# Attention, soft mixture and second layer on one core: last tile's scores moved up, unread products taken out, loads paced earlier, running maximum kept per slot and place

## The chip, the cores and the metric

The kernel runs on one core of one Trainium2 chip. The metric is the device time of one execution in microseconds (us), as the median of the runs shown. The engines have short names: PE is TensorE (PEld its weight loads), DVE VectorE, ACT ScalarE, POOL GpSimd; SP is the engine that only issues transfers here. Each takes its instructions in the order of the program and waits on semaphores for the others. PSUM is the memory that PE writes, SBUF the large memory beside the engines.

## The reference

Three layers follow one another. Attention within chunks of 64 places, a soft mixture of 8 experts with 4 slots each (so 32 slots), and a layer with a softmax unit, a normalisation and two weights:

```python
scores = scale * q_c @ k_c^T; attn = softmax(scores); x = attn @ v_c      # 4608 tokens of 512
logits = x @ phi                                                          # 4608 x 32
d = exp(logits - logits.max(0)); d /= d.sum(0) + 1e-09                    # over the tokens
slot_input = d.T @ x                                                      # 32 x 512
slot_out[e] = relu(slot_input[e] @ w1[e]) @ w2[e]                         # 8 experts
c = softmax(logits, over the slots); x = c @ slot_out
h = x @ w_in; solu = h * softmax(h); out = layernorm(solu) * g_ln @ w_out
```

The maximum over all 4608 tokens is not known while they come; the kernel keeps a running maximum and multiplies the sums so far by the exponent of the difference (`al`) whenever a block of four tiles is added.

## The kernel before, in words

The 4608 tokens are 36 tiles of 128, and four tiles are a block (9 blocks). Tiles 0 to 33 run through a software pipeline of 34 steps. In step i the letters of a row of `STEP` (row i mod 4) say in which order the pieces of work are written, and so in which order each engine gets them: `S` (scores of tile i, 16 products), `mx` and `sub` (maximum and subtraction, DVE), `exp` (ACT), `PT` and `PTe` (transposes of the tile before and their copy out of PSUM by ACT), `x` (products with v of tile i-2), `rz`, `rc`, `xm` (row sums by ACT, reciprocal and multiplication by DVE), `xT` and `xTe` (transposes of tile i-3 and their copy by ACT). Letters `t`, `m`, `u`, `a`, `add`, `mul`, `sq` turn the second layer's weights from their raw form, and `qk`, `v`, `raw`, `W` issue loads on SP.

Once in four steps a block is folded in: `LT` makes the logits of four tiles in PSUM (32 slots by 4 places in the partitions, 128 tokens along the row), `lte` copies them to the SBUF tile `ltb`, `L` transposes them, `lall` stores them, `tm` takes the running maximum along the row, `mT` transposes that maximum, `mn`, `d`, `mc` (DVE) take the maximum over the four places, subtract it and pick it into a column, `de` (ACT) takes the exponent in place and `al` the factor for the older sums; `z` multiplies the exponents with ones on PE to get their sum, `sl` multiplies them with the tiles, and `acc` adds both to the running sums on DVE.

The expert weights are 64 loads of 512 KB on SP's queue. 23 of them have a place in `ring` from the start; `PACE[i]` says how many are issued by step i. The others go to places that other tiles leave (`own_c`, `own_q`, `own_v`, `own_p`, `own_t`, `own_x`) and to `ring` places that were used up.

Tiles 34 and 35 and everything up to the second layer are written out in `ORDER`: names with the operations they stand for, which are checked to come after what they need, and are otherwise issued as listed. `S34`, `S35` are the scores, `mx`, `sub`, `exp`, `PT`, `ptev`, `x`, `rz`, `ev`, `xT`, `xtev`, `LT` follow for each tile (tile 35 in two halves, 350 and 351; `ev` is reciprocal and multiplication). `lte8`, `L8`, `tm8`, `mT8`, `mn8` are the last block without its last tile, `lte83`, `Ls`, `L83`, `mnl` that tile; `mb` spreads the maximum, `d7`, `d8`, `de7`, `de8`, `sl70` to `sl81`, `z8`, `acc80`, `acc81`, `zt`, `si0`, `si1`, `siT` give the slots' inputs. `id0` to `id6` (line 646) are 13 instructions of products of the unit matrix with itself into PSUM places that nobody reads then; PE runs each of them in two passes.

Then the experts: `w1_000` to `w2_111` and `wc48` to `wc63` are PE's products with the 64 weight loads. Beside them the second layer is prepared: `cm0` and `cm1` are the mean of `w_out` on PE, `cme` its copy to SBUF on DVE, `cms0` to `cms7` subtract it on POOL (line 834), `px0` to `px7` take maxima of the results on DVE (line 1059), `px8` and `wmt` collect them (PE, line 1071), and `wmv`, `hi`, `lo` split the weights by that scale. `cz0` to `cz5` is the other softmax on DVE and ACT (lines 889 to 899). From about 187 us a loop over the 36 tiles runs the second layer with PE back to back to the end; nothing of it is touched.

## Time and profile before

| | before |
|---|---|
| median of 3 runs | 404.35 us (404.04 to 406.44) |
| the profiled execution | 406.2 us, of which 404.4 us span from first to last instruction |
| mean granted TensorE clock | 0.999 |
| PE busy in the span | 385.9 us (95%) |
| DVE, ACT, POOL busy | 311.5, 223.8, 199.4 us |
| transferred | 99.20 MB, of that 70.60 MB read from HBM |

The profile is one execution on the chip. Times in its rows count from the first instruction. A row of the timeline stands for one instruction or several merged ones, and says how long its engine sat idle before it and for whom. Ends of products on PE are modelled, so the start of the next row says more than a duration.

### The profile page before, as it was taken

What the parts mean: (1) busy time and instruction counts of PE and PEld (TensorE: products, weight loads), DVE (VectorE), ACT (ScalarE), POOL (GpSimd) and SP (SyncE); (2) the same over time, 40 slices, a digit from 0 to 9 for tenths busy, and PEclk for the clock granted to TensorE, in tenths of its full rate; (3) what the DMA queues carried; (4) which work ended last, traced back from release to release, by engine and by line L of the source; (5) the groups of instructions that cost most, each with busy time, mean ns of one, the idle gap of its engine ahead of it and who ended that gap; (6) DMA issues with size and microseconds to landing.
All of it is one profiled execution on the core that took longest, in us unless ns stands there. A gap on an engine that the chain in (4) does not pass through costs nothing. (4 is left out here: it accounts for less than half of the span.)

```text
span 404.4 us, 10343 instructions
## 1 busy us (share of the span) xinstructions
PE 385.9 (95%) x3961; PEld 223.0 (55%) x3961; DVE 311.5 (77%) x777; ACT 223.8 (55%) x470; POOL 199.4 (49%) x201
## 2 busy tenths in 40 slices
PE   3798999999999999999999999999999999999997
PEld 2676777877787752355544444444444444444445
DVE  3588788888987447683989789999888888888840
ACT  1487777877776512231576765556545545455521
POOL 2377677777778428240113235555545445454430
PEclk9999999999999999999999999999999999999999
DMA  7999999999999999993056756778657786567661
GB/s 231 361 411 409 407 407 408 409 397 387 403 361 347 404 398 402 408 410 82 15 98 151 130 134 140 166 166 160 144 132 135 156 130 143 133 143 156 131 157 52
DMA packets 101153, 99.20 MB, mean 245 GB/s; under 512 B 78064, under 2 KB 78704, under 8 KB 101104
## 3 DMA queue, kind: packets, MB, share of 16 engines
q1 hardware_dynamic: 101104, 98.54, 77.9%
q8 instruction: 31, 0.51, 0.5%
q14 instruction: 18, 0.15, 0.1%
HBM read 70.60 MB, written 9.44 MB: 198 GB/s over the span
## 5 line engine op out<-in xcount | busy, mean ns | idle before, releaser
L1197 POOL TENSOR_SCALAR uh<-u,sc 128x1024 f16<-128x1024 f32 (+1 forms) x35 | 65.0, 1857 | 51.2 <-issue 38.3
L1396 PEld LDWEIGHTS <-uhT 128*128 128x128 f16 x560 | 52.2, 98 | 68.6 <-issue 9.0
L1396 PE MATMUL o_ps<-xb,uhT 128*128 128x512 f16 x280 | 66.6, 380 | 0.8 <-DMA uhT<-uh 0.8
L1396 PE MATMUL o_ps<-xb,ulT 128*128 128x512 f16 x280 | 66.3, 379 | 0.0
L1396 PE MATMUL o_ps<-wo,uhT 128*128 128x512 f16 x280 | 66.1, 379 | 0.0
L1325 ACT ACTIVATE e<-h_ps,nm 128x1024 f32<-128x1024 f32 x34 | 37.8, 1112 | 43.9 <-DVE nm L1319 43.9
L1213 ACT ACTIVATE e<-u,nmean 128x1024 f32<-128x1024 f32 x35 | 40.1, 1147 | 28.7 <-DVE nmean L1212 28.7
L257 PE MATMUL s_ps<-qk 128*64 128x128 f32 x576 | 42.4, 291 | 10.8 <-DMA qk<-in_qkT 7.3
L1363 POOL TENSOR_TENSOR a<-a,mhalf 128x1 f32<-128x1 f32 x36 | 21.7, 604 | 56.6 <-DVE a L1380 42.7
L1319 DVE TENSOR_REDUCE nm<-h_ps 128x1 f32<-128x1024 f32 x34 | 41.5, 1220 | 9.7 <-PE h_ps L1314 9.7
L1188 DVE SCALAR_TENSOR_TENSOR u<-h_ps,e 128x1024 f32<-128x1024 f32 x35 | 42.8, 1223 | 6.1 <-ACT e L1325 6.1
L1396 PEld LDWEIGHTS <-ulT 128*128 128x128 f16 x280 | 27.3, 98 | 33.1 <-issue 0.3
L1373 DVE SCALAR_TENSOR_TENSOR ul<-u,sc,uh 128x1024 f16<-128x1024 f32 x35 | 45.3, 1295 | 0.0
L257 PEld LDWEIGHTS s_ps<-qk 128*64 128x64 f32 x576 | 33.1, 144 | 17.9 <-issue 12.1
L266 DVE TENSOR_REDUCE mx<-s_ps 128x8 f32<-128x512 f32 x36 | 24.7, 685 | 12.5 <-PE s_ps L257 12.3
L399 ACT ACTIVATE xt_b<-xt_ps 128x512 f32<-128x512 f32 (+1 forms) x37 | 21.5, 584 | 17.3 <-PE xt_ps L417 16.5
L220 POOL TENSOR_SCALAR conv<-conv 128x256 f32<-128x256 f32 x16 | 17.5, 1096 | 24.6 <-ACT conv L207 24.6
L1414 ACT ACTIVATE ob<-o_ps,a 128x512 f32<-128x512 f32 x35 | 23.7, 678 | 9.5 <-PE o_ps L1396 8.0
L1314 PE MATMUL h_ps<-s,c4T 128*128 128x512 f32 x68 | 27.6, 488 | 0.0
L278 ACT ACTIVATE p<-p 128x512 f32<-128x512 f32 x35 | 21.7, 620 | 6.7 <-DVE p L272 6.7
L272 DVE TENSOR_TENSOR p<-s_ps,mx 128x512 f32<-128x512 f32 x35 | 24.1, 690 | 0.9
L230 POOL TENSOR_TENSOR conv<-conv 128x256 int32<-128x256 int32 x32 | 23.3, 727 | 2.6
(234 smaller groups left out, 637.8 us busy)
## 6 DMA issues: line engine op xcount, KB each, us to landing
w<-in_w SPq DMA_DIRECT2D x45, 512.0 KB, 8.3
qk<-in_qkT SPq DMA_DIRECT2D x72, 256.0 KB, 7.0
vall<-in_v SPq DMA_DIRECT2D x18, 520.0 KB, 7.6
out<-ob SPq DMA_DIRECT2D x35, 256.0 KB, 2.1
raw<-in_w SPq DMA_DIRECT2D x16, 512.0 KB, 7.6
qk<-in_w SPq DMA_DIRECT2D x4, 512.0 KB, 9.6
w_raw<-in_w SPq DMA_DIRECT2D x3, 512.0 KB, 9.3
vall<-in_w SPq DMA_DIRECT2D x3, 512.0 KB, 9.0
```

The source lines that it names most:

```text
L257: nc.tensor.matmul(s[ts(c, 64), ts(g, 128)], b[:, 1, ts(2 * g + c, 64)], b[:, 0:3:2, ts(2 * g + c, 64)], start=True, stop=True, tile_posit ...
L266: mark("mx", nc.vector.tensor_reduce(out=mx, in_=s, axis=AX.X, op=ALU.max))
L272: mark("sub", nc.vector.tensor_tensor(out=p, in0=s, in1=mx.unsqueeze(2).to_broadcast([128, 8, 64]), op=ALU.subtract,))
L1188: nc.vector.scalar_tensor_tensor(out=u, in0=d["h"], scalar=1.0, in1=e, op0=ALU.mult, op1=ALU.mult, accum_out=zz[:, 1:2])
L1197: nc.gpsimd.tensor_scalar(out=uh[:, 0:n], in0=u[:, 0:n], scalar1=d["sc"][:, 1:2], scalar2=1.0, op0=ALU.mult, op1=ALU.mult)
L1213: nc.scalar.activation(out=d["e"], in_=d["u"], func=AF.Square, bias=nmean, scale=1.0, accum_out=d["zz"][:, 2:3])
L1314: nc.tensor.matmul(h[:, ts(n, 512)], c4T[:, i, :], s4[n], start=True, stop=True)
L1319: nc.vector.tensor_reduce(out=nm, in_=st[i]["h"], axis=AX.X, op=ALU.max, negate=True)
L1325: nc.scalar.activation(out=d["e"], in_=d["h"], func=AF.Exp, bias=d["nm"], scale=1.0, accum_out=d["zz"][:, 0:1])
L1373: nc.vector.scalar_tensor_tensor(out=ul, in0=d["u"], scalar=d["sc"][:, 1:2], in1=d["uh"], op0=ALU.mult, op1=ALU.subtract)
L1396: nc.tensor.matmul(d["o"], lt(n % 8), w(n % 8), start=(n == 0), stop=(n == 23))
L1414: nc.scalar.activation(out=ob, in_=d["o"], func=AF.Copy, scale=d["a"][:, 7:8])
```

## The change

Six things are done.

`S35`, the scores of tile 35, and `mx35` stand directly behind `S34` and `mx34`, and the list around them is reordered. The products `id0` to `id6` are gone. `PACE` is higher from its 19th number on.

In the pipeline the running maximum stays per slot and place: the block's logits are stored with their sign turned, `tm` becomes a minimum along the row into one of two columns in turn, and the exponent `e` is taken by ACT from `ltb` one step earlier, directly behind `lall`, with its sum `z` from the same instruction and with `al` behind it. PE then transposes the exponents (`eT`) where it transposed the maximum, and `de` is a copy out of PSUM. `mn`, `d`, `mc` on DVE and the product `z` on PE are gone in blocks 0 to 6.

The last two blocks need one maximum for the four places together. For that `ml` is stored, `ml4` on POOL spreads it over four columns by a mask `msk` (a DVE reduction at the start), and `mT8` gets one more product; a DVE maximum in `mn8` goes.

In `ORDER` `cm1` moves from ahead of `w1_000` to behind `w1_001`, and on DVE `d7` and `acc80` go ahead of `mc` and `zacc8`.

```diff
 PACE = [
-    0, 0, 1, 1, 2, 3, 3, 4, 4, 5, 6, 6, 7, 7, 8, 9, 9, 10, 10, 11, 12, 12, 13, 13, 14, 15, 15, 16,
-    16, 17, 18, 18, 19, 22, 25, 25,
+    0, 0, 1, 1, 2, 3, 3, 4, 4, 5, 6, 6, 7, 7, 8, 9, 9, 10, 11, 11, 12, 13, 14, 14, 15, 16, 16, 17,
+    18, 19, 19, 20, 21, 23, 25, 25,
...
-hz0 sl71 de8 al sl70 own_x z8 sl80 zacc8 sl81 zt acc80 acc81 zr si0 si1 siT open2 cm1 w1_000 w1_001 cme rl00 w1_010
+acc80 sl81 own_x zacc8 acc81 zt si0 si1 zr siT open2 w1_000 w1_001 cm1 cme rl00 w1_010 cz0 cms2 cms3 ht00 w1_011 he00
...
+    msk = kvp.tile([128, 4], F32, name="msk")
+    nc.vector.tensor_reduce(out=msk, in_=ident.rearrange("p (t s) -> p t s", t=4), axis=AX.X, op=ALU.add)
...
-    nc.gpsimd.memset(ltm[:, 128:129], -3.0e38)
+    nc.gpsimd.memset(ltm[:, 128:130], 3.0e38)
...
+    def sign(b):
+        return -1.0 if b < last - 1 else 1.0
+
+    def low(b):
+        return ltm[:, 128 + b % 2:129 + b % 2]
...
-        nc.vector.tensor_reduce(out=ltm[:, 128:129], in_=ltm[:, 0:129], axis=AX.X, op=ALU.max)
+        nc.vector.tensor_reduce(out=low(b), in_=ltm[:, 0:130], axis=AX.X, op=ALU.min)
...
-    def mTm(b):
-        blk_s[b]["mT"] = t = ps1.tile([128, 160], F32, tag="m", name="mT_ps")
-        nc.tensor.transpose(t[:, 0:128], ltm[:, 128:129].to_broadcast([128, 128]), ident)
...
+    def ex(b):
+        st = blk_s[b]
+        st["z"] = z = sm.tile([128, 1], F32, tag="z", name="z", bufs=2)
+        st["e"] = e = t2.tile([128, 128], F32, tag="e", name="e", bufs=1)
+        nc.scalar.activation(out=e, in_=ltm[:, 0:128], func=AF.Exp, scale=-1.0, bias=low(b), accum_out=z)
+        if b > 0:
+            st["al"] = al = sm.tile([128, 1], F32, tag="al", name="al", bufs=1)
+            nc.scalar.activation(out=al, in_=low(b - 1), func=AF.Exp, scale=-1.0, bias=low(b))
...
+    def eT(b):
+        st = blk_s[b]
+        st["eT"] = t = ps1.tile([128, 128], F32, tag="m", name="eT_ps")
+        nc.tensor.transpose(t, st["e"], ident)
...
+        V(E("de"))(d, st["eT"].rearrange("p (t s) -> p t s", t=4))
...
-    def zm(b):
-        st = blk_s[b]
-        st["z"] = lt_t[b][:, 3, 0:1]
-        nc.tensor.matmul(st["z"], st["d"].rearrange("p t s -> p (t s)"), ones, start=True, stop=True)
...
-    op("id0", "PT350")(lambda: idle(T["pt"][:, 2, :], 2))
...
+        T["mT"] = ps1.tile([32, 132], F32, tag="m", name="mT_ps")
+        nc.tensor.transpose(T["mT"][:, 0:128], blk_s[last]["tm"], ident)
+        nc.tensor.matmul(T["mT"][:, 128:132], istack, T["ml4"], start=True, stop=True)
...
-        nc.vector.tensor_tensor(out=mn, in0=mn, in1=blk_s[last - 2]["mc"][0:32], op=ALU.max)
```

How the order moves is seen on PE at the end of the pipeline. Ahead of these rows stand the 33 earlier tiles; `s_ps` is written by `S34` and `S35`, `pt_ps` by the transposes of probabilities, `x_ps` by the products with v, `xt_ps` by `xT31` and `lt_ps` by `LT31`. Before:

```order
L257 MATMUL s_ps<-qk_113 64x128 x8
L417 MATMUL xt_ps<-cs,xb_83 128x128 x4
L408 MATMUL pt_ps<-cs,p 128x128 x4
L283 MATMUL x_ps<-vall,pt 64x65 x16
L326 MATMUL lt_ps<-xt_b,phi_sb 32x128 x16
L257 MATMUL s_ps<-qk_114 64x128 x8
L408 MATMUL pt_ps<-cs,p 128x128 x4
```

In the change, the same place:

```order
L258 MATMUL s_ps<-qk_113 64x128 x8
L258 MATMUL s_ps<-qk_114 64x128 x8
L424 MATMUL xt_ps<-cs,xb_83 128x128 x4
L415 MATMUL pt_ps<-cs,p 128x128 x4
L284 MATMUL x_ps<-vall,pt 64x65 x16
L327 MATMUL lt_ps<-xt_b,phi_sb 32x128 x16
L284 MATMUL x_ps<-vall,pt 64x65 x16
L415 MATMUL pt_ps<-cs,p 128x128 x4
```

`S35` has passed four pieces of work, and `x33` now stands ahead of `PT34`.

The second place is PE where the experts begin: `zt`, the two `si`, `cm1`, then the products with the weights. Before:

```order
L846 MATMUL zt_ps<-cs,zacc 128x32
L857 MATMUL s_ps<-cs,acc 128x32 x4
L827 MATMUL cm_ps<-csum,mean_l 128x256
L939 MATMUL h_ps_2581<-w,xl_152 4x512 x16
L939 MATMUL h_ps_2582<-w,xl_152 4x512 x8
```

In the change:

```order
L838 MATMUL zt_ps<-cs,zacc 128x32
L849 MATMUL s_ps<-cs,acc 128x32 x4
L931 MATMUL h_ps_2552<-w,xl_154 4x512 x16
L819 MATMUL cm_ps<-csum,mean_l 128x256
L931 MATMUL h_ps_2553<-w,xl_154 4x512 x8
```

`cm1`, the product into `cm_ps`, now stands behind sixteen products with the experts' weights.

The third is ACT in the step that folds a block in. Before, `lall`, then `rz`, `xTe` and `PTe`:

```order
L361 ACTIVATE lall<-L_ps 128x128
L305 ACTIVATE rz<-x_ps 128x8
L399 ACTIVATE xt_b<-xt_ps 128x512
L399 ACTIVATE pt<-pt_ps 128x512
```

In the change:

```order
L368 ACTIVATE lall<-L_ps 128x128
L441 ACTIVATE e,z<-ltb 128x128
L444 ACTIVATE al<-ltb 128x1
L306 ACTIVATE rz<-x_ps 128x8
L406 ACTIVATE xt_b<-xt_ps 128x512
L406 ACTIVATE pt<-pt_ps 128x512
```

Two instructions, `e` with its sum and `al`, have come between.

## Rows read from the trace of the kernel before

**Rows 1.** Busy time by stretch: from:to, length, PE, PEld, DVE, ACT, POOL, clock, DMA share, GB/s.
```profile
20.00:88.00 68.00, 64.40 (x1277) 50.34 (x1275) 58.21 (x143) 51.13 (x133) 50.43 (x60) 1.00 1.03 408
116.00:128.00 12.00, 11.77 (x210) 9.12 (x205) 10.43 (x28) 8.60 (x23) 9.60 (x12) 1.00 0.90 318
148.10:167.28 19.18, 19.18 (x174) 5.30 (x173) 13.53 (x20) 3.95 (x7) 11.07 (x8) 1.00 1.04 404
184.00:185.00 1.00, 1.00 (x40) 0.75 (x31) 0.41 (x3) 0.00 (x0) 0.00 (x0) 1.00 0.62 115
```
**Rows 2.** Waits: what PE's scores waited for; us in total, times, longest us.
```profile
PE s_ps L257 <- DMA qk<-in_qkT: 7.3, 2, 5.2
```
**Rows 3.** PE's timeline, one block: start, us, engine, line, operation [idle before <-for].
```profile
82.11 1.07 PE L468 MATMUL sl_ps<-xb,d 128*32 128x512 f32 x8 [0.24 <-ACT d L449]
83.11 0.38 PE L462 MATMUL lt_ps<-cs,d 128*128 128x1 f32 x2
83.35 0.64 PE L417 MATMUL xt_ps<-cs,xb 128*128 128x128 f32 x4
```
**Rows 4.** ACT's timeline in that block, and the PE row behind the copy `pt`.
```profile
77.48 0.60 ACT L399 ACTIVATE pt<-pt_ps 128x512 f32<-128x512 f32 x1
...
81.77 0.29 ACT L449 ACTIVATE d<-d 128x128 f32<-128x128 f32 x1
81.97 0.28 ACT L457 ACTIVATE al<-mc 128x1 f32<-128x1 f32 x1
...
78.39 0.70 PE L283 MATMUL x_ps<-vall,pt 64*64 64x65 f32 x32
```
**Rows 5.** Timeline of PE, then one row of DVE and of ACT, last two tiles.
```profile
126.02 1.09 PE L257 MATMUL s_ps<-qk 128*64 128x128 f32 x16
129.70 1.09 PE L257 MATMUL s_ps<-qk 128*64 128x128 f32 x16
143.26 0.61 PE L646 MATMUL s_ps<-cs 128*128 128x128 f32 x4
143.80 1.07 PE L687 MATMUL sl_ps<-xb,ltb 128*32 128x256 f32 x16
...
127.88 0.69 DVE L272 TENSOR_TENSOR p<-s_ps,mx 128x512 f32<-128x512 f32 x1
...
138.98 0.49 ACT L346 ACTIVATE ltb<-lt_ps 128x384 f32<-128x384 f32 x1 [1.39 <-PE lt_ps L646]
```
**Rows 6.** PE's timeline early in the execution, behind idle time.
```profile
13.82 1.98 PE L257 MATMUL s_ps<-qk 128*64 128x128 f32 x16 [2.06 <-DMA qk<-in_qkT]
...
38.38 1.09 PE L257 MATMUL s_ps<-qk 128*64 128x128 f32 x16 [1.17 <-DVE mT_ps L429]
```
**Rows 7.** PE, DVE and POOL where the experts begin and weights are prepared.
```profile
147.49 0.68 PE L827 MATMUL cm_ps<-csum,mean_l 128*128 128x256 f32 x2
148.10 5.33 PE L939 MATMUL h_ps<-w,xl 128*4 128x512 f32 x48
...
147.69 0.29 DVE L863 TENSOR_TENSOR xl<-s_ps,zr 128x128 f32<-128x128 f32 x1 [0.25 <-PE s_ps L857]
...
154.67 1.76 DVE L890 TENSOR_TENSOR lall<-lall,cz 128x1152 f32<-128x1152 f32 x1
156.35 1.27 DVE L1059 TENSOR_REDUCE wmx<-wo 128x1 f32<-128x512 f32 x2
165.26 0.15 DVE L1066 TENSOR_REDUCE wmx<-wmx 128x1 f32<-128x8 f32 x1
...
148.98 9.82 POOL L834 TENSOR_TENSOR wo<-wo,acc 128x512 f32<-128x512 f32 x7 [13.19 <-DVE acc L400]
...
155.15 2.42 POOL L834 TENSOR_TENSOR wo<-wo,acc 128x512 f32<-128x512 f32 x1
```
**Rows 8.** The queue of loads: the last tile's issues, and the median landing.
```profile
118.38 1.69 SPq L177 DMA_DIRECT2D qk<-in_qkT  x2
...
qk<-in_qkT SPq DMA_DIRECT2D x72, 256.0 KB, 7.0
```

More of the change, by code (lines that the diff above doesn't have):

```diff
@@ L45 @@
 ORDER = """
-cq1 cq2 cq3 cq4 cq5 cq6 cq7 S34 loadw xT31 PT33 xtev31 x32 own_c mx34 rz32 LT31 sub34 ev32 S35 ptev33 lte7 mx35 exp34
-sub350 PT34 x33 ptev34 xT32 L7 exp350 rz33 xtev32 own_q sub351 x34 ev33 PT350 exp351 id0 rz34 ptev0 xT33 PT351 LT32
-lall7 tm7 x350 ptev1 x351 xtev33 ev34 xT34 LT33 id1 xtev34 own_v rz35 rc35 LT34 id2 ev350 ev351 xT350 px lte8 xT351
-id4 xtev350 xtev351 L8 tm8 LT35 id5 mT8 lte83 mn8 own_p Ls L83 id6 own_t mnl hz1 lall83 mb lall8 cm0 mc id3 d7 d8 de7
-hz0 sl71 de8 al sl70 own_x z8 sl80 zacc8 sl81 zt acc80 acc81 zr si0 si1 siT open2 cm1 w1_000 w1_001 cme rl00 w1_010
@@ L51 @@
-cz0 cms2 cms3 ht00 w1_011 he00 cms6 cz1 cms4 rl01 px2 w2_000 cms7 ht01 px7 w2_001 cms0 cz2 cz3 px6 cz4 cms5 px3 cz5
-he01 w2_010 w2_011 so0 px4 px5 cms1 w1_100 px1 w1_101 px0 sot0 late ch0 cl0 px8 wmt ch2 cl2 wmv ct0 ch1 w1_110 rl10
-cl1 hi0 ct1 ch3 hi1 lo0 ht10 he10 ch4 cl3 ce0 hi6 ce1 ct2 ce2 w1_111 cpt cpe rl11 ch5 wc48 hi3 ct3 ht11 hi4 cl4 ce3
-hi5 wc49 hi7 cl5 ct4 lo3 wc50 wc51 ch6 he11 ce4 cl6 wc52 wc53 lo2 ct6 wc54 wc55 ch8 ct5 hi2 ce6 soc0 wc56 soe0 wc57
-ch7 soct0 cl7 ct7 ce5 ce7 wc58 cl8 wc59 soce0 wc60 wc61 soc2 soct2 wc62 wc63 soc3 lo1 sw0 soct3 soce2 sw1 soce3 sw2
@@ new lines @@
+x33 own_q PT34 ptev34 xT32 L7 ml4 rz33 sub351 sub350 x34 exp350 PT350 exp351 ev33 xtev32 ptev0 xT33 PT351 lall7 LT32 rz34
+x350 ptev1 ev34 xtev33 xT34 x351 xtev34 rz35 LT33 rc35 LT34 ev350 ev351 tm7 lte8 px xT350 xT351 own_v L8 tm8 xtev350
+xtev351 LT35 lte83 mT8 mn8 own_p Ls own_t L83 mnl lall8 lall83 hz1 mb d7 mc de7 al cm0 d8 de8 sl70 hz0 sl71 sl80 z8
+acc80 sl81 own_x zacc8 acc81 zt si0 si1 zr siT open2 w1_000 w1_001 cm1 cme rl00 w1_010 cz0 cms2 cms3 ht00 w1_011 he00
+cms6 cz1 cms4 rl01 px2 w2_000 cms7 ht01 px7 w2_001 cms0 cz2 cz3 px6 cz4 cms5 px3 cz5 he01 w2_010 w2_011 so0 px4 px5
@@ L641, in soft_moe_kernel @@
         lambda: LT_mm(lt_t[last], 3))
-    def idle(o, n):
-        for _ in range(n):
-            nc.tensor.matmul(o, ident, ident, start=True, stop=True)
-    op("id0", "PT350")(lambda: idle(T["pt"][:, 2, :], 2))
-    op("id1", "LT33 id0")(lambda: idle(lt_t[last][:, 3, :], 2))
-    op("id2", "LT34 id1")(lambda: idle(lt_t[last][:, 3, :], 2))
-    op("id4", "xT351 ev34 id2")(lambda: idle(sx[:, 0, 256:384], 1))
-    op("id5", "LT35 id4")(lambda: idle(sx[:, 0, 256:384], 1))
-    op("id6", "L83 lte8 id5")(lambda: idle(lt_t[last][:, 0, :], 2))
-    op("id3", "cm0 mnl ev34 id2")(lambda: idle(sx[:, 0, 256:384], 2))
     op("lte7", "LT31")(lambda: blk_a(last - 1))
@@ L721, in mT8, with ml4 @@
     def mT8():
-        T["mT"] = ps1.tile([32, 128], F32, tag="m", name="mT_ps")
-        nc.tensor.transpose(T["mT"], blk_s[last]["tm"], ident)
-    op("mT8", "tm8")(mT8)
+        T["mT"] = ps1.tile([32, 132], F32, tag="m", name="mT_ps")
+        nc.tensor.transpose(T["mT"][:, 0:128], blk_s[last]["tm"], ident)
+        nc.tensor.matmul(T["mT"][:, 128:132], istack, T["ml4"], start=True, stop=True)
+    def ml4():
+        T["ml4"] = m4 = sm.tile([128, 4], F32, tag="m4", name="ml4", bufs=1)
+        nc.gpsimd.tensor_scalar(out=m4, in0=msk, scalar1=blk_s[last - 2]["ml"], scalar2=1.0, op0=ALU.mult, op1=ALU.mult)
+    op("ml4")(ml4)
+    op("mT8", "tm8 ml4")(mT8)
     def mnv8():
```

55 lines of the change are left out of this document (23 added, 32 removed).

## The prediction

> **What bounds the kernel now.** First the busy time by stretch. From 20 to 88 us, inside the pipeline, PE is busy for 64.40 of 68 us and the transfers fill their engines (share 1.03, 408 GB/s) [rows 1]. Two engines are therefore full at once, and the reader has to ask which of them holds the other up. The waits answer it: PE's score products waited for loads only twice, 7.3 us in all, the longer wait 5.2 us, at the start [rows 2]. Later on, PE does not stand still for a load, so PE sets the pace and the loads keep up with it. PE's own timeline of one block shows one real pause, 0.24 us ahead of `sl`, for the exponent `d` from ACT; the next rows touch [rows 3]. Hence an instruction taken off PE in the pipeline is worth its whole slot, and one taken off DVE, ACT or POOL is worth nothing unless PE waits for it.
>
> In the last two tiles this is different. There are too few independent pieces, and PE fills its time with products that nobody reads: four passes of them from 143.26 to 143.80, and ACT's copy `lte8` sat idle for 1.39 us behind others of them [rows 5]. This stretch is bound by a chain from engine to engine. From 148.10 to 167.28 PE is busy all 19.18 us with the experts [rows 1], so it is the bound again, and at the end of that stretch stands `wmt`, which must not come before DVE's `px8`.
>
> The profiled execution took 406.2 us, 1.85 above the median of 404.35, and the places below last some 0.1 to 6 us each. I use its differences, not its total, and put the sum on the median.
>
> **The loop.** The product `z` leaves PE in seven blocks: it starts at 83.11 and the next work at 83.35, a slot of 0.24 [rows 3], so 7 x 0.24 = 1.68 less. The maximum's transpose is replaced by one of the same form, so nothing changes there. `mn`, `d` and `mc` leave DVE, but PE's only pause in the block is for ACT, so that is worth nothing. ACT gains two instructions ahead of `rz`, `xTe` and `PTe`. The exponent of the same shape takes 0.20 until the next one starts (81.77 to 81.97), and `al` is at most 0.28 long [rows 4]; reading out the sum of `e` has no row, and I take it to be inside these 0.48. The copy `pt` (`PTe`) starts at 77.48 and lasts 0.60; the product that needs it starts at 78.39 [rows 4]. If all 0.48 reach it, it ends at 78.56, 0.17 late, seven times 1.2. If only the 0.28 reach it, it ends at 78.36 and is hidden. ACT is busy for 51.13 of 68 us [rows 1], so a part will fall into its pauses; I take 0.01 per block, 0.1 in all. `de` becomes a copy at the same place of ACT's order, behind the same instructions, so the 0.24 pause ahead of `sl` stays. Loop: **-1.6**; bounds -0.5 (0.17 late each time) and -3.4 (the pause goes too, 7 x 0.24 more).
>
> **The last two tiles.** `S35` stands at 129.70 and moves to behind `S34` at 126.02 [rows 5]. By itself this buys little: all pieces between the two move back by its slot of about 1.02, and on DVE `mx35` now stands ahead of `sub34`, which starts at 127.88 [rows 5] and comes about 0.9 later. Tile 34 is late by that, tile 35 early; the chain needs both. The unread products are 13 instructions of two passes, 26 x 0.54 / 4 = 3.5 us of PE's slots [rows 5]. Where they stood in front of work that was ready, their time comes back; where they stood in front of a wait, only the cover goes. Following the new list with the slots of the old rows, `lte8` comes 1.1 earlier (its 1.39 us of waiting nearly go), and what is behind it is mostly one chain, transposition, maximum, exponent, sums, whose links keep their length. I take **-1.0**; bounds 0 and -3.5.
>
> On the unread products there is a rule against the change, and the trace has a row on each side of it. At 13.82, behind 2.06 us of idle time, 16 score products took 1.98; at 38.38, behind 1.17 us, they took 1.09 [rows 6]. The granted clock reads 1.00, the level of 2.4 GHz, in every stretch that I read [rows 1]. The Trainium skill ("TensorE: Matmul & The Clock Gate", section "What's actually happening") says that the engine's default is the throttled state and that activity releases it, so it would have the unread products hold the clock up. By the row at 38.38 the sum stands as it is; by that rule, with the slow row for a price, it is the second rival below.
>
> **The experts.** `cm1` filled 147.49 to 148.10, but DVE's `siT`, for which the first expert product waits, only started at 147.69 and lasted 0.29 [rows 7]: its 0.61 were cover, and moving it gives nothing there. Behind `w1_001` they are a slot of their own: +0.61. And it makes POOL late. Let W be the start of the experts (148.10 before). POOL's sums start at 148.98, so W + 0.88, that is 0.88 behind the end of `cm1` [rows 7]. Now `cm1` ends behind 16 instructions or 32 of the 48 passes that take 5.33 [rows 7], at W + 3.55 + 0.61, and the sums start at W + 5.04. Five of them take 155.15 - 148.98 = 6.17, the sixth 2.42 beside DVE's long `cz1` (154.67, 1.76 us), against 1.23 for each of the five [rows 7]. This collision now falls among the first five: +1.2, the fifth ends at W + 12.4, and its maximum `px7` (half of 1.27 us [rows 7]) at W + 13.0. Behind `px7` DVE worked without a pause from 157.62 to 165.41, the end of `px8` [rows 7], 7.8 us: `px8` ends at W + 20.8. PE comes to `wmt` at W + 19.18 [rows 1] + 0.61 = 19.8, so it waits about 1.1. Experts: **+1.7**; bounds +0.6 (collision hidden) and +2.9 (two sums hit).
>
> **The loads.** From 116 to 128 us the transfers ran at 318 GB/s instead of the 404 that they reach beside full PE work [rows 1]; 86 GB/s over 12 us are 1.0 MB, or 2.6 us of transfer at 404 GB/s, that the raised pace can bring in earlier. But at the end of the experts the transfers have already run down (115 GB/s at 184 to 185 us [rows 1]) while PE is fully busy, so earlier loads are hidden anyway: 0.
>
> **Small ones.** The mask `msk` lies in the time ahead of the first score, when PE waits for its load; `ml4` waits on POOL in front of nothing that PE needs before the experts; one more product in `mT8` is at most the slot of two passes, 0.24 [rows 3], and a maximum on DVE goes in exchange: 0 together.
>
> Sum: -1.6 - 1.0 + 1.7 = -0.9, from 404.35 to about 403.5.
>
> **Rivals.** (1) POOL's late start is absorbed: the order behind `px7` has slack, `wmt` costs only the slot of 0.61. Then -1.6 - 1.0 + 0.6 = -2.0, 402.3; if in addition all 3.5 us of the unread products come back, 399.8. For it: the collision is a single row. Against it: DVE stood gapless behind `px7`. (2) Slower: without the unread products PE's clock falls in the last stretch before the experts, 143.80 to 148.10, 4.3 us of work [rows 5, 7]. The slow row costs 0.89 more per 1.09 [rows 6], so 4.3 us cost 3.5, and the sum becomes +2.6, 407.0. It decides from 1.1 us of slow work on (1.1 x 0.82 = 0.9). For it: such a row exists. Against it: 1.17 us of idle time left the pace alone, and the waits here are shorter. (3) The scores of tile 35 wait for their load. It is issued at 118.38 and lands 7.0 later by the median, 125.4 [rows 8]; `S35` would be reached at 127.0 less the loop's 1.6, also 125.4, and the raised pace puts loads of up to 2.6 us in front of it. With half of that PE waits 1.3: 404.7. For it: the queue is full. Against it: the issue itself moves up with the loop.
>
> **How the numbers follow.** My forecast has 0.47, the first rival 0.24 (0.09 of it near 399.8), the second 0.12, the third 0.17. The likeliest gives 403.5, alone from 402.3 to 404.5. Down to 400.9 some 0.08 is left out, mostly the far end of the first rival; up to 406.5 some 0.10, the second at its full price. About 1%, 4.0 us, is what a measurement of this kernel can tell from no change: below 400.3 lies the far end of the first rival, with a little for the loop's bound, 0.10; above 408.4 the second rival with the third or the experts' upper bound, 0.06; within 0.84.
>
> **What would show it.** In the changed profile one block of the pipeline is 0.24 shorter and the product behind `PTe` has no new pause; `lte8` no longer shows 1.39 of waiting; the first expert product starts about 2.6 us earlier; `wmt` then comes 1.7 later behind it, with a pause on PE put down to DVE. A row of 16 score-like products at twice 1.09 in that stretch would speak for the second rival, a wait of `S35` on its load for the third. The forecast is wrong if `wmt` follows the experts without a pause or if the first expert product is not earlier by 1.5 us at least.

## The result, and the profile after

The changed kernel takes 410.62 us (median of 6 runs, 408.83 to 415.41), the kernel before 405.43 us (median of 6, 404.04 to 406.44). The ratio is 1.0122 with a 95% interval of 1.0095 to 1.015: the change makes the kernel slower, by about 5 us. I had forecast 403.5, from 400.9 to 406.5 (0.9 less than 404.35, the median of the three runs then known), and had given "slower by over 1%" a chance of 0.06. The ratios in this document leave out runs in a slower state, over 1.5% above the fastest of the same kernel, as that of 415.41 here. The spread of the runs after is itself a finding: the kernel before stays within 2.4 us, the changed one does not, and the mean granted clock of an execution tells where in the spread it lies (1.000: 408.8 and 408.9; 0.996: 410.1; 0.992: 411.1 and 412.8; 0.983: 415.4).

The profiled execution after took 410.14 us, with a span of 408.4, against 406.2 and 404.4. These 4.0 us come apart by four rows that both traces have. S34 is the first score product of the last two tiles, W the first expert product.

| stretch of PE | before | after | difference | forecast |
|---|---|---|---|---|
| start to S34 | 126.02 | 127.14 | +1.1 | -1.6 |
| S34 to W | 22.08 | 20.97 | -1.1 | -1.0 |
| W to `wmt` | 19.18 | 21.54 | +2.4 | +1.7 |
| `wmt` to the second layer's first products | 22.68 | 24.38 | +1.7 | 0 |
| from there to the end | 214.4 | 214.3 | 0 | 0 |

So in these two traces one of four terms had its sign wrong, one was too small, and one was missing. The first row is the least sure: other traces of the unchanged loop reach S34 at 124.97 and 125.08 instead of 126.02, and those of the changed one between 124.54 and 128.38. By my own sign the forecast fails in any case: the first expert product starts at 148.11, where 148.10 less 2.6 was forecast. PE's timeline after, at W and at `wmt`, shows the third (start, us, engine, line, operation, idle time before it and for whom):

```profile
127.14 1.97 PE L258 MATMUL s_ps<-qk 128*64 128x128 f32 x32
...
148.11 2.33 PE L931 MATMUL h_ps<-w,xl 128*4 128x512 f32 x20 [0.48 <-DVE xl L855]
...
169.65 0.32 PE L1063 MATMUL wm_ps<-cs,wmx 128*128 128x128 f32 x1 [1.46 <-DVE wmx L1058]
170.36 0.66 PE L914 MATMUL c_ps<-cs,cc 128*128 128x128 f32 x4 [0.39 <-DVE isw L1066]
170.95 1.51 PE L931 MATMUL h_ps<-xb,xl 128*4 128x512 f32 x8
172.21 1.95 PE L931 MATMUL h_ps<-w,xl 128*4 128x512 f32 x8
```

PE waits 1.46 us ahead of `wmt`, where before it waited for nothing [rows 1, 7]. The last two rows are eight passes each; in the kernel before such rows lasted 1.04. The busy time by stretch after says why (from:to, length, then PE, PEld, DVE, ACT, POOL, the granted clock, DMA share, GB/s):

```profile
168.00:170.00 2.00, 0.51 (x3) 0.13 (x1) 1.90 (x6) 0.60 (x1) 0.00 (x0) 1.00 1.01 401
170.00:172.00 2.00, 1.64 (x12) 0.68 (x16) 1.33 (x5) 0.60 (x1) 0.00 (x0) 0.85 1.04 410
172.00:174.00 2.00, 2.00 (x12) 0.17 (x4) 0.00 (x0) 0.00 (x0) 1.41 (x3) 0.50 1.01 406
174.00:176.00 2.00, 1.75 (x14) 1.42 (x11) 0.89 (x2) 0.60 (x1) 2.00 (x4) 0.80 1.04 412
176.00:178.00 2.00, 2.00 (x20) 0.63 (x22) 2.00 (x4) 0.60 (x1) 2.00 (x2) 1.00 1.01 404
```

PE was busy for 0.51 of 2 us, and right behind that the clock was granted at 0.50, its level of 1.2 GHz, and was back at 1.00, 2.4 GHz, from 176 us on. That is the fourth row of the table.

What made `wmt` late is on DVE and POOL after:

```profile
152.39 0.69 DVE L407 COPY acc<-cm_ps 128x512 f32<-128x512 f32 x1 [4.43 <-PE cm_ps L819]
...
160.55 0.69 DVE L1051 TENSOR_REDUCE wmx<-wo 128x1 f32<-128x512 f32 x1 [3.06 <-POOL wo L826]
...
163.01 1.27 DVE L887 TENSOR_SCALAR cz<-cz 128x36 f32<-128x36 f32 x1
...
169.44 0.15 DVE L1058 TENSOR_REDUCE wmx<-wmx 128x1 f32<-128x8 f32 x1
...
153.17 11.06 POOL L826 TENSOR_TENSOR wo<-wo,acc 128x512 f32<-128x512 f32 x8 [15.80 <-DVE acc L407]
```

POOL begins at W + 5.06 (148.98, or W + 0.88, before [rows 7]), DVE stands idle for 3.06 us for the sum that `px7` needs, and `px8` starts at 169.44.

The loop is the surprise. A block of four steps, from `sl` to `sl`, in PE's timeline after:

```profile
68.78 1.07 PE L468 MATMUL sl_ps<-xb,d 128*32 128x512 f32 x8 [0.15 <-ACT d L406]
...
77.62 1.09 PE L258 MATMUL s_ps<-qk 128*64 128x128 f32 x16
78.84 0.79 PE L284 MATMUL x_ps<-vall,pt 64*64 64x65 f32 x32
...
82.59 1.07 PE L468 MATMUL sl_ps<-xb,d 128*32 128x512 f32 x8 [0.18 <-ACT d L406]
```

From 68.78 to 82.59 are 13.81 us; the block before ran from 68.30 to 82.11 [rows 3], also 13.81. The product `z` and its 0.24 are gone, and nothing was gained. Two slots have grown. The one from the scores to `x`, 1.02 before (77.37 to 78.39), is 1.22 here. And `LT`, the logits of the block, has become longer, in the kernel before and in the change:

```profile
68.30 1.07 PE L468 MATMUL sl_ps<-xb,d 128*32 128x512 f32 x8
...
73.35 1.25 PE L326 MATMUL lt_ps<-xt_b,phi_sb 128*32 128x128 f32 x32
```

```profile
73.47 1.38 PE L327 MATMUL lt_ps<-xt_b,phi_sb 128*32 128x128 f32 x32
```

The 0.20 and the 0.13, less 0.06 at `sl`, eat the 0.24. From `LT` to the next scores are 1.31 in nearly every block of the new loop in all its traces, also where `x` is not late, and 1.18 in that of before; the cause of these 0.13 is open. ACT's timeline of the same place has what stands ahead of the copy that `x` needs:

```profile
76.80 0.28 ACT L368 ACTIVATE lall<-L_ps 128x128 f32<-128x128 f32 x1 [0.53 <-PE L_ps L364]
76.97 0.39 ACT L441 ACTIVATE e<-ltb 128x128 f32<-128x128 f32 x1
77.27 0.19 ACT L441 ACTIVATION_READ_ACCUMULATOR e<-ltb 128x1 f32 x1
77.36 0.28 ACT L444 ACTIVATE al<-ltb 128x1 f32<-128x1 f32 x1
77.54 0.16 ACT L306 ACTIVATE rz<-x_ps 128x8 f32<-128x8 f32 x1
77.60 0.59 ACT L406 ACTIVATE xt_b<-xt_ps 128x512 f32<-128x512 f32 x1
78.08 0.60 ACT L406 ACTIVATE pt<-pt_ps 128x512 f32<-128x512 f32 x1
```

`e`, the reading of its sum and `al` fill 76.97 to 77.54: 0.57 us. The copy `pt` ends at 78.68, and `x` starts at 78.84.

Last, PE has four pauses in the loop after that end with no event that the profile knows, called "issue":

```profile
32.21 0.41 PE L327 MATMUL lt_ps<-xt_b,phi_sb 128*32 128x128 f32 x3 [1.20 <-issue]
...
52.35 0.38 PE L424 MATMUL xt_ps<-cs,xb 128*128 128x128 f32 x2 [1.11 <-issue]
...
92.06 0.88 PE L258 MATMUL s_ps<-qk 128*64 128x128 f32 x12 [0.19 <-issue]
...
104.86 0.27 PE L284 MATMUL x_ps<-vall,pt 64*64 64x65 f32 x2 [0.68 <-issue]
```

They sum to 3.18 us, and they cut groups of equal products in two (29 passes of `LT`, then 3). No pause of that name stands in the loop of the kernel before, but one of 0.46 at the same kind of place stands there under another (last section).

### The profile page after: what moved, and what is told of

The parts are those of the page before. It is cut to its first block, busy times and chain, and to the rows that moved or that the text cites. A ratio compares the mean times of both kernels' runs of the same rounds, so it can differ in the third digit from the quotient of the medians.

```text
span 408.4 us, 10257 instructions
## 1 busy us (share of the span) xinstructions
PE 385.2 (94%) x3925; PEld 219.6 (54%) x3925; DVE 312.4 (76%) x749; ACT 225.4 (55%) x485; POOL 199.7 (49%) x202
## 5 line engine op out<-in xcount | busy, mean ns | idle before, releaser
L284 PE MATMUL x_ps<-vall,pt 64*64 64x65 f32 x1088 | 24.5, 227 | 2.0 <-ACT pt L406 0.7
```

Of the source, the lines that this page charges most:

```text
L284: nc.tensor.matmul(x[ts(c, 64), a, ts(g, 65)], pt[ts(a, 64), ts(c, 64)], vall[ts(a, 64), i % 6, ts(2 * g + c, 65)], start=True, stop=True, ...
```

## The experiments

Theory A had three parts: the moved `cm1` makes PE wait at `wmt`; behind such a wait the clock falls; and `e` and `al` stand in the way of `PTe`. Its rivals were that the missing unread products, the raised pace or the place of `S35` did it. Each median stands beside that of the kernel before on the same chip, which lay between 405.17 and 405.95 throughout.

**cm1 put back.**

```diff
-siT open2 w1_000 w1_001 cm1 cme
+siT open2 cm1 w1_000 w1_001 cme
```

> The changed kernel with one thing undone: cm1 stands ahead of w1_000 again. Theory A (the late sums on POOL make PE wait 1.46 us at wmt, and behind that pause the clock falls to 0.50 of its level for some 4 us): wmt comes 19.2 us behind the first expert product instead of 21.5, no pause there, no stretch below 1.00 between 168 and 178 us, mean granted clock 0.999 or more in every run; time 2.4 + 1.7 = 4 us under the changed kernel's profiled execution, about 406, and the runs scatter less. Rival B (the clock falls because the unread products of the last tiles are gone, wherever PE waits): the pause goes, 2.4 us are gained, but some runs still have a mean clock of 0.996 or less.

Measured: 406.67 (403.54 to 408.82, 12 runs), 1.0033 of the kernel before (1.0006 to 1.0061): 3.95 less than the whole change. PE's timeline of this kernel:

```profile
145.50 5.33 PE L931 MATMUL h_ps<-w,xl 128*4 128x512 f32 x48
...
164.67 0.27 PE L1063 MATMUL wm_ps<-cs,wmx 128*128 128x128 f32 x1
```

19.17 us and no wait. The first part of theory A holds, in size too. But four of the twelve executions still had a mean clock of 0.996, and these took 408.4 on average, against 405.6 for the other eight: rival B has its share, the clock can fall without the wait at `wmt`.

**cm1 moved in the kernel before, and nothing else.** The same diff the other way round.

> The kernel before with cm1 moved behind w1_001 and nothing else. Theory A: wmt comes 21.5 us behind the first expert product, 2.3 us later than before, with a pause on PE of some 1.5 us; time 2.4 us above the kernel before where the clock stays at 1.000, 4 where it falls to 0.50 behind the pause; median 407.5 to 409.5. Rival C (the late sums cost only with the rest of the change): within 1 us of the kernel before.

Measured: 408.40 (406.78 to 410.57, 6 runs), ratio 1.0088 (1.0064 to 1.0112). `wmt` waits 1.47 us. The three executions at a clock of 1.000 mean 407.6, 2.4 above the kernel before; the three at 0.996 mean 409.2, 1.6 more. The move costs this by itself, with no help from the rest; the kernel before, run beside all these experiments, was at or below 0.996 in 2 of 105 executions.

**Products in the wait.** Ten passes that nobody reads directly ahead of `wmt`, in the changed kernel.

```diff
+        for _ in range(5):
+            nc.tensor.matmul(t, ident, ident, start=True, stop=True)
         nc.tensor.transpose(t, mx[:, 8:9].to_broadcast([128, 128]), ident)
```

> The changed kernel with ten passes of products that nobody reads (1.35 us) put into PE's pause directly ahead of wmt; nothing else. Theory A: wmt does not come earlier (21.5 us behind the first expert product), but the clock stays at 1.00 behind it; 1.7 us less than the changed kernel's profiled execution, about 408.4 in every run, mean clock 0.999 or more. Rival C (the fall has nothing to do with this pause): the clock falls as before, mean 0.992 to 0.996 in half of the runs, and no time is gained.

Measured: 409.91 (407.40 to 415.26, 6 runs), ratio 1.01 (1.0077 to 1.0123), no sure gain over the change. In the trace the wait shrinks to 0.35 and the clock stays at 1.00 behind it, as theory A says; that is one execution, and the mean clocks of the six, 0.983 to 1.000, scatter as those of the change do. It fell at another place instead, in the last two tiles, by the busy time of this kernel:

```profile
140.00:142.00 2.00, 1.70 (x9) 1.15 (x8) 1.22 (x7) 0.93 (x4) 0.00 (x0) 0.84 1.04 395
142.00:144.00 2.00, 2.00 (x18) 0.79 (x20) 0.08 (x1) 0.98 (x4) 0.00 (x0) 0.50 1.01 400
144.00:146.00 2.00, 2.00 (x24) 0.88 (x16) 0.63 (x2) 0.00 (x0) 0.00 (x0) 0.81 1.04 389
...
148.00:150.00 2.00, 2.00 (x12) 0.35 (x8) 0.00 (x0) 0.00 (x0) 0.00 (x0) 0.55 1.02 395
```

There are thus two places where the clock falls in some executions: behind the wait at `wmt`, and between 140 and 152 us, where the unread products had stood.

**The unread products put back, with cm1 put back too.** All of them behind the same products as before (`id0`, `id5`, `id6`, `id3` in the lines left out). They are twelve instructions, not the 13 that the forecast and the expectations name: the trace of before has 24 passes of line 646, two for each.

```diff
-x350 ptev1 ev34 xtev33 xT34 x351 xtev34 rz35 LT33 rc35 LT34 ev350 ev351 tm7 lte8 px xT350 xT351 own_v L8 tm8 xtev350
+x350 ptev1 ev34 xtev33 xT34 x351 xtev34 rz35 LT33 id1 rc35 LT34 id2 ev350 ev351 tm7 lte8 px xT350 xT351 id4 own_v L8 tm8 xtev350
...
```

> The changed kernel with two things undone: the unread products id0 to id6 stand where they stood between the last tiles' work, and cm1 is ahead of w1_000 again. Theory G (without the unread products PE has enough idle time between 136 and 146 us for the clock to fall to 0.50 in some executions, 1.7 us a time; a PE pause at wmt does the same): mean granted clock 0.999 or more in every run, against 4 of 12 runs at 0.996 with cm1 alone put back; no time above 407; median 404.5 to 406, that is the kernel before within 1 us, since the tail then loses the 1.1 us that it had gained. Rival H (the clock falls for another reason, such as the loads' pace or the order of S35): some runs at 0.996 or less as before.

Measured: 409.53 (408.51 to 410.12, 4 runs), ratio 1.0112 (1.0096 to 1.0128). The clock was 1.000 in all four, as theory G says, but the time went up by 2.9. PE's timeline of this kernel, at both ends of the last two tiles:

```profile
127.61 1.97 PE L258 MATMUL s_ps<-qk 128*64 128x128 f32 x32
...
150.78 5.33 PE L943 MATMUL h_ps<-w,xl 128*4 128x512 f32 x48
```

23.17 us, 2.2 longer than without them and 1.1 longer than before the change: in the new order of the list they stand in front of work that is ready. (The rest is in the loop, where this execution had pauses of 0.98 and 1.23 at 103.70 and 112.63.) So in the new order the removal of the products is worth 2.2 in this stretch, and the order with `S35` ahead, taken with them, is a loss of 1.1. In theory G's forecast the time was 404.5 to 406; that part missed.

**The unread products put back, cm1 left where the change has it.** The lines above without the cm1 diff.

> The changed kernel with the unread products put back and cm1 left where the change has it. Theory G: no fall of the clock between 138 and 152 us in the profile, but the pause of 1.5 us ahead of wmt stays, and behind it the clock falls in some executions; run clocks 0.996 to 1.000, none below; time 2.4 us above the same kernel with cm1 back where the clock is 1.000, 4 where it is 0.996. Rival H: clocks of 0.983 to 0.992 still occur.

Measured: 412.99 (409.34 to 414.69, 6 runs), ratio 1.0175 (1.0134 to 1.0217). No fall between 138 and 152 us; the wait of 1.47 at `wmt` and a granted clock of 0.50 behind it, from 176 to 178, are there. No execution was under 0.996: one fall at most, as theory G says. The price holds only in part: the four executions at 0.996 mean 413.6, 4.1 above the 409.5 with `cm1` back, as forecast, but the two at 1.000 mean 409.4, where 2.4 above it was forecast. The "issue" pauses differ too, 4.54 us in this trace and 2.81 in that one.

**The unread products left out of the kernel before.**

```diff
-    op("id0", "PT350")(lambda: idle(T["pt"][:, 2, :], 2))
...
-    op("id3", "cm0 mnl ev34 id2")(lambda: idle(sx[:, 0, 256:384], 2))
```

> The kernel before with its 13 unread products left out, and nothing else changed. Theory G: runs with a mean clock of 0.996 or less occur, each fall costing 1.7 us; in runs at 1.000 the time is 0 to 1.5 us under the kernel before, since ACT no longer waits 1.39 us behind them; median 0 to 2 us above the kernel before. Rival H: clock 1.000 in every run, time 1 us under the kernel before.

Measured: 406.08 (404.72 to 410.53, 12 runs), ratio 1.0032 (1.0007 to 1.0056). The last two tiles last 21.21 us (125.08 to 146.29), 0.9 less than before, and one of twelve executions had a clock of 0.996, with 410.53. Between the theories: falls occur, but rarely here, and the time is not under the kernel before. In the trace the 0.9 go again behind `wmt`: from there to the second layer's first products are 23.69 us instead of 22.68, with an "issue" pause of 0.48 at 183.28 among them, and the rest of the execution is 0.6 longer. So in the old order the removal is worth 0.9, and without the products the new order is only 0.24 shorter than the old (20.97 against 21.21).

**e and al moved back behind PTe.**

```diff
-t m a S x u raw L tm v mx xT add qk PT lall e rz mul xTe sub rc PTe W sq xm exp
+t m a S x u raw L tm v mx xT add qk PT lall rz mul xTe sub rc PTe e W sq xm exp
```

> The changed kernel with the exponent e and al moved behind PTe in ACT's order (both in the same step of the pipeline). Theory A (e with its sum and al take 0.57 us ahead of PTe, so that the product x behind it is late by about 0.2 us per block, which eats the slot of the removed product z): the 0.18 us pauses ahead of x go, a block of four steps without other pauses lasts 13.6 instead of 13.8 us, S34 starts 1.2 to 1.5 us earlier, time 1.2 to 1.5 us under the changed kernel. Rival D (the block is held by something else, as the transfers): the pause moves to the next place and S34 starts at the same time within 0.3 us.

Measured: 409.79 (408.48 to 410.28, 5 runs), ratio 1.0113 (1.0097 to 1.013), the change as a whole being at 1.0122. The pauses ahead of `x` are gone, but PE's timeline of this kernel has them elsewhere:

```profile
67.80 1.06 PE L468 MATMUL sl_ps<-xb,d 128*32 128x512 f32 x8 [0.68 <-ACT d L406]
...
81.88 1.07 PE L468 MATMUL sl_ps<-xb,d 128*32 128x512 f32 x8 [0.54 <-ACT d L406]
```

A block now lasts 14.08, and S34 comes at 127.20, where it was 127.14. Rival D is right about the place: ACT's own chain through the step holds the block, and what is taken from in front of `PTe` comes out in front of `sl`.

**e and al ahead of lall, with cm1 put back.** ACT had a pause of 0.53 there; that is where the work can go.

```diff
-t m a S x u raw L tm v mx xT add qk PT lall e rz mul xTe sub rc PTe W sq xm exp
+t m a S x u raw L tm v mx xT add qk PT e lall rz mul xTe sub rc PTe W sq xm exp
```

> The changed kernel with cm1 back ahead of w1_000, and with e and al directly ahead of lall instead of behind it (e needs only the minimum of the block, which DVE has 0.6 us before ACT may write lall; ACT stood idle there for 0.53 us). Against the same kernel without this move. Theory A (PTe is late by what e and al take ahead of it): the pauses of 0.18 us ahead of the product x go, a block without other pauses lasts 13.55 instead of 13.8 us, 1.2 us over five blocks, time 1.2 us less at the same clock. Rival D (ACT's whole work of a block is the limit, and a pause only moves): the pause ahead of sl grows by what the one ahead of x loses, a block stays at 13.8 us.

Measured: 403.91 (403.16 to 404.88, 6 runs), ratio 0.995 (0.9933 to 0.9966). This version beats both kernels. PE's timeline of this kernel, an early block:

```profile
52.41 1.06 PE L468 MATMUL sl_ps<-xb,d 128*32 128x512 f32 x8
...
65.81 1.06 PE L468 MATMUL sl_ps<-xb,d 128*32 128x512 f32 x8
```

13.40 us, 0.4 under a block of the kernel before, with no pause ahead of `sl`, and `x` is back at a slot of 1.02: both of the pauses that ACT made are gone. The median fell by 2.8 against `cm1` alone, by about 2 where only executions at a clock of 0.999 or more are compared. That this is 0.4 in each of seven blocks is not shown: the next four blocks of the profiled execution last 14.20 to 14.50, with waits for loads and "issue" pauses, and S34 comes at 125.16, later than the 124.54 of the trace with `cm1` alone. Over the traces the kernels with `e` ahead and the usual start reach it at 124.05 to 125.16 (three), those with `e` behind `lall` and the raised pace at 124.54 to 128.38 (five).

**The old pace.** The change with the old numbers of `PACE`.

> The changed kernel with the old numbers of PACE. Theory E (the raised pace fills the transfers from 88 to 128 us, and PE's pauses that wait for nothing the profile shows, 0.68 and 0.19 us at 92 and 105 us, come from it): those pauses of that stretch go, 0.9 us less at S34. Rival F (these pauses fall where they fall, whatever the pace): as many and as long, S34 within 0.3 us of the changed kernel; and the loads of the experts still land in time, so the time is the same within 0.5 us.

Measured: 410.07 (409.40 to 413.59, 6 runs), ratio 1.0146 (1.0113 to 1.0179). Two pauses are left between 20 and 126 us, 0.35 and 0.72; the one at 102.88 stays. No time was gained in the median. In the trace S34 comes at 125.19, 1.95 earlier than in that of the change, more than theory E's 0.9, but the clock falls twice, at 147 and 171 us; and the raised pace has reached S34 as early in other traces. So the pace is not shown to have made the change slow.

**The new pace in the kernel before.** Only `PACE` changed.

> The kernel before with the raised PACE and nothing else. As predicted: earlier loads are hidden, time within 0.5 us of the kernel before. Theory K: the transfers fill the stretch from 88 to 128 us, pages of code land later, and up to 1 us is lost in pauses of PE between 88 and 126 us.

Measured: 404.62 (404.17 to 407.12, 12 runs), ratio 0.9979 (0.9962 to 0.9996). No "issue" pause behind 31 us, although the transfers ran at 404 to 408 GB/s all the way to 124. As predicted the pace is worth little; here it gains 0.9 rather than nothing. A full transfer system alone does not make the pauses.

**A pace so low that the transfers are not full.** The change with `cm1` back and `PACE` held at 6 from the 12th step.

> The changed kernel with cm1 back ahead of w1_000, and PACE kept at 6 loads from the 12th step to the end of the pipeline, so that 13 loads of 512 KB come later: a probe of the pipeline alone, the experts may have to wait. Theory K (PE's pauses that wait for nothing the profile shows are its own code, 16 KB pages that come over the same full transfer engines as the loads and land up to 1.2 us late): with the transfers well under 400 GB/s between 60 and 116 us, those pauses at 83 to 113 us are gone, and a block of four steps lasts 13.7 to 13.9 us each time, against up to 15.5 before. Rival L (they come from the place of the instructions): pauses of 0.2 and 0.7 us at the same two instructions as in every other trace of the changed loop.

Measured: 422.07 (418.97 to 422.91, 5 runs), ratio 1.0406 (1.0386 to 1.0426): the experts wait for their loads, as the probe had to. In the loop the busy time of this kernel is:

```profile
60.00:88.00 28.00, 27.34 (x559) 21.18 (x559) 24.89 (x57) 21.88 (x62) 21.32 (x25) 1.00 0.91 320
88.00:116.00 28.00, 27.33 (x557) 21.14 (x550) 24.87 (x56) 21.58 (x61) 21.70 (x25) 1.00 0.85 290
```

and there is no "issue" pause at all; five blocks last 69.1 us, against 70.6 with `cm1` alone put back, where the pauses were 0.18, 0.26 and 0.68. Theory K needs this and rival L cannot have it: without full transfers the pauses are gone at the very same instructions.

**Three unread products.** The fastest version with one each at the three places where PE is idle anyway.

```diff
+    op("id2", "LT34")(lambda: idle(lt_t[last][:, 3, :], 1))
+    op("id6", "L83 lte8 id2")(lambda: idle(lt_t[last][:, 0, :], 1))
+    op("id3", "cm0 mnl ev34 id2")(lambda: idle(sx[:, 0, 256:384], 1))
```

> The changed kernel with cm1 back and e, al ahead of lall, and with three of the thirteen unread products put back, one each at the places where PE then stands idle anyway: ahead of the transposes of tile 35 (0.41 us idle), ahead of mb (0.30) and behind cm0 (0.16). Theory G (a few idle places of the last tiles let the clock fall now and then; what the products cost is only what they take beyond those pauses): mean granted clock 1.000 in all runs against 0.996 in 2 of 6 without them; the last two tiles, S34 to the first expert product, last 21.0 to 21.2 us as without them; median 403.2 to 404.2, 0.3 to 0.5% under the kernel before. Rival M (three products are too few to hold the clock, or stand in the way of ready work like all thirteen, which lengthened this stretch by 2.2 us): falls still occur, or the stretch lasts over 21.7 us and the time is over 404.5.

Measured: 406.98 (405.39 to 409.39, 9 runs), ratio 1.0052 (1.0028 to 1.0076). The last two tiles last 21.01 us, so the products themselves cost nothing there, as theory G says; but the median is 3 us above the fastest version's, five of nine executions were at 0.996, so three do not hold the clock (rival M), and the profiled execution has the longest of these pauses in any trace:

```profile
184.28 0.64 PE L990 MATMUL h_ps<-w,xb 128*4 128x128 f32 x15 [2.08 <-issue]
```

**Products at the very start.** The fastest version, and the kernel before, with 16 or 32 products of one column ahead of the first score, to move the later pages of PE's code.

```diff
+    for _ in range(16):
+        nc.tensor.matmul(sx[:, 1, 0:1], ident, ones, start=True, stop=True)
```

> The fastest kernel so far (the change with cm1 back and e, al ahead of lall) with 16 products of one column that nobody reads at the very start, where PE waits for its first load: they move every later page of PE's code by a quarter. Theory P (where a page boundary falls decides whether the page lands in time): the pauses without a named cause move to other instructions and their sum changes by 0.5 us or more, and the time with it, by 1 to 3 us either way. Rival Q (the pauses belong to the loop's work and the full transfers): the same sum within 0.5 us, time within 0.5 us of 403.9.

> The same with 32 products, half a page. Theory P: other places again, and another time, 1 to 3 us off. Rival Q: as without.

> The kernel before with the same 16 products at the start. Theory P: the kernel before owes some of its time to where its pages lie; pauses without a named cause appear in the loop or the experts, and the time is 1 to 3 us above it. Rival Q: within 0.5 us of the kernel before.

> The same with 32 products. Theory P: 0 to 3 us above the kernel before, and not the same as with 16. Rival Q: within 0.5 us of it.

Measured, in this order: 405.49 (0.9996, 0.9975 to 1.0017), 413.19 (1.0175, 1.0136 to 1.0214), 407.94 (1.0057, 1.0031 to 1.0083) and 415.36 (1.0236, 1.0198 to 1.0274). The totals decide nothing, since the probe was not free: at the start PE runs these products slowly, and the first score product comes at 9.9 or 16.7 us instead of 5.2 to 5.4. What the traces do show is that the pauses move. In the fastest version they stand at 83.95, 90.22, 102.96 and 116.91 us (1.76 in all, behind 30 us); with 16 products, and with 32:

```profile
64.42 0.88 PE L260 MATMUL s_ps<-qk 128*64 128x128 f32 x12 [0.19 <-issue]
...
77.11 0.33 PE L286 MATMUL x_ps<-vall,pt 64*64 64x65 f32 x2 [0.58 <-issue]
```

```profile
56.02 0.33 PE L286 MATMUL x_ps<-vall,pt 64*64 64x65 f32 x3 [0.76 <-issue]
```

Other instructions, and 0.77 and 0.76 in all. Of the kernel before, the trace with 16 products has no such pause behind 30 us, against theory P, and the one with 32 has three, 0.94 in all. Theory P holds for the places; for the sum it is open, as the late start also gives the loads a lead.

**The fastest version with the old pace.**

> The change with cm1 back and e, al ahead of lall, and with the old numbers of PACE. Theory K (code pages land late behind full transfers): the pauses between 83 and 117 us shrink from 1.8 to under 0.8 us, time 0.5 to 1 us less than with the raised pace, 402.9 to 403.4, if the loads of the experts still come in time. Rival R (the faster loop itself needs all transfers, whatever the pace): the loop waits as long as before, time 403.9 or, with the loads later, up to 1.5 us more.

Measured: 404.25 (402.47 to 406.65, 12 runs), ratio 0.9971 (0.9948 to 0.9993). Its pauses between 83 and 103 us sum to 1.86, no shorter than with the raised pace (1.27 there, 1.76 up to 117): the two paces differ for the transfers only behind 116 us (287 against 388 GB/s up to 124). Rival R holds; with either pace the faster loop wants all of the transfers (399 to 408 GB/s from 60 to 116 us here).

## Why the prediction was wrong, step by step

**What bounds the kernel: right, but read too far.** PE is the bound of the loop, and an instruction taken off it is worth its slot only where no other engine is just as late. The single pause of the block, 0.24 for ACT [rows 3], was the sign that ACT's chain was already behind PE there. I read it as a constant.

**The loop: forecast -1.6, measured 0 in the blocks and +1.1 at S34.** The step that failed is "I take 0.01 per block, 0.1 in all", with its reason that a part would fall into ACT's pauses. ACT's additions are 0.57, not 0.48, as the reading of the sum has a slot of its own (0.09), and `x` came 0.20 to 0.28 late in six of the seven blocks, about 1.5 in all: past the bound of 0.17 that I had worked out and put aside. The slot of `z` itself did come free; what was left of it went into the 0.13 of `LT`, which had no term. The nearest pause of ACT stood ahead of `lall`, on the wrong side of the new work; only the kernel with `e` and `al` ahead of `lall` uses it, and there a block can be 13.40, where 13.57 was forecast. `de` behind `PTe`'s neighbours was right, the pause ahead of `sl` stayed (0.15 and 0.18). The +1.1 at S34 is no clean figure: the "issue" pauses, which had no place in the sum, are 3.18, against them stand waits that only the trace of before has (1.17 at 38.38 [rows 6], 0.46 and 0.51 later), and S34 moves by 1 us between traces of the unchanged loop.

**The last two tiles: forecast -1.0, measured -1.1.** The size is right, and so is the link: `lte8` waits 0.54 instead of 1.39 and comes 11.85 behind S34 instead of 12.96. The split between the two steps was not worked out: with the products the order costs 1.1, without them it gains 0.24, and removing them gains 0.9 in the old order and 2.2 in the new. They are 12 instructions, so my 3.5 us of slots are 3.2.

**The experts: forecast +1.7, measured +2.4.** The mechanism was the one forecast, link by link: POOL starts at W + 5.06 (5.04 forecast), and `px7` ends at W + 13.1 (13.0). The mis-sized term is DVE's stretch behind it: "7.8 us" became 8.4, since the 128x36 scaling in it took 1.27 instead of 0.57 (its duration in the trace of before). POOL's last sum runs beside it both times, so why it did is open. The wait was 1.46 against 1.1, and PE itself came 0.3 later to `wmt`.

**The clock: the second rival, 0.12, came true in kind, at a place that I had not named and, in traces of other versions, near the one that I had.** The fall behind `wmt` follows a wait that my own sum contained: I had priced 1.1 us of idle time and not asked what it does to the clock. My argument against the rival, that 1.17 us of idle time left the pace alone [rows 6], was one row; `wmt` shows 1.46 and 0.39 with one product between them. My slow row, at 13.82, was no fall behind a pause at all: in the trace of before PE's products run at that pace up to some 18 us, also those with no pause ahead of them:

```profile
16.80 1.11 PE L408 MATMUL pt_ps<-cs,p 128*128 128x128 f32 x4
...
20.06 0.60 PE L408 MATMUL pt_ps<-cs,p 128*128 128x128 f32 x4
```

Five traces have a wait of 1.46 or 1.47 at `wmt`. In four of them the clock falls right behind it, in the fifth, the kernel with `e` behind `PTe`, it does not; in none of the fourteen others does it fall there. One fall goes with 0.004 of mean clock and lengthens its stretch by 1.7 us (24.38 against 22.68), half of the 3.5 that I had priced. That the falls follow the moved `cm1` is shown; that they come from PE's idle time rests on the one trace with products in the wait. For the last tiles, with `cm1` in its old place: 10 of 48 executions of kernels in the new order without the products were at 0.996 or less, and none of 34 of kernels that have them, but only four of these 34 are in the new order. So the products or the order hold the clock, and the products are the likelier cause, not the shown one. How many are needed, and why the kernel before without them fell only once in twelve, stays open.

The Trainium skill ("TensorE: Matmul & The Clock Gate", section "What's actually happening") has activity release a throttle that is the default; the rows at 172 us, half the clock behind a stretch with 0.51 of 2 us busy, agree with it, and I had set it aside too lightly.

**The loads: forecast 0, measured 0 to -0.9.** Right in kind. The opposite direction is not hidden: 13 loads issued late cost 15 us. The third rival, `S35` waiting for its load, did not happen in any trace of the new order; `S34` and `S35` run as one row of 32 passes without a pause.

The balance: by the medians, undoing the two misplaced steps gives back 3.95 (`cm1`) and 2.8 (`e` and `al`), the second of which no pair of traces shows in full, and what is left of the change is 0.5% faster than the kernel before, 2.0 us. That this is also the -2.0 of my first rival is luck: that rival had `cm1` moved and `e` behind `lall`.

## What to carry to other kernels

When work is moved onto an engine that is not the bound, look for the pause that it is to fill and put it on that side of the queue: the same 0.57 us left a block at 13.81 behind `lall` and let it be 13.40 ahead of it. A filler moved away from a wait is worth nothing there and its full slot elsewhere, and whatever waits for its result moves with it. A new wait on PE should be priced with the clock that may fall behind it, 1.7 us a time here, and not by its length alone.

## What the runs showed of the hardware

PE's code comes in pages over the same transfer engines as the data, and can be late. In the trace after, the transfers by queue in 29 to 30 us and in 102.3 to 102.6 us (queue, kind: packets, MB, share of 16 engines) are:

```profile
q1 hardware_dynamic: 115, 0.39, 97.2%
q8 instruction: 1, 0.02, 6.7%
```

```profile
q1 hardware_dynamic: 32, 0.12, 102.3%
q8 instruction: 1, 0.02, 23.1%
```

One instruction packet each, 1.1 us long (0.067 x 16 x 1.0, and 0.231 x 16 x 0.3), so that they end before 31.1 and at about 103.5; PE goes on at 32.21 and 104.86. The two pauses at 52.35 and 92.06 have such a packet ahead of them too. That alone says little, as one comes every 6 to 8 us there. Counting settles it. When every record of PE in the trace is counted (products, weight loads and those of its sequencer), 705, 1473, 3009 and 3521 stand ahead of the four pauses: 3, 6 and 2 times 256 apart, and a packet has 16,384 bytes, 64 for each of 256 records. In the 19 traces, 45 of the 49 "issue" pauses between 20 and 190 us stand behind 449 + 256 k records, and each ends 1.2 to 1.6 us behind the end of instruction packet k, counted from 0; the other four are at 20 and 24 us in the kernels with 32 products at the start. At none of these places does PE go on sooner than 1.2 us behind its packet, pause or not. Together with the probe of the low pace (no pauses) and the moved products (other places), this shows that the pauses are late code, under full transfers. The loop of the kernel before is not free of it: the pause at its record 1473, 1.38 behind a packet, is only put down to PE's own `x`.

```profile
51.70 0.60 PE L417 MATMUL xt_ps<-cs,xb 128*128 128x128 f32 x4 [0.46 <-PE x_ps L283]
```

Where a page ends can thus be counted; which one comes late differs from execution to execution. The Trainium skill ("Runtime: NRT & Kernel Launch", section "Instruction fetch mechanics") tells of 16 KiB blocks that the sequencer fetches while it runs the block before, at a cost that is mostly hidden. The packets of 0.02 MB agree; hidden it was not: 3.18 us in one execution here, and 2.08 at a single boundary.

That has a consequence for measuring: in five traces with the same loop and the same pace (the change, and the kernels with `cm1` back, with products in the wait, and with the unread products back) these pauses sum to 1.12 to 4.54 us behind 20 us, so a small difference between two versions needs a look at these pauses before it is put down to the work that was changed.
